# Transposing all four ds tiles of a block by DMA, and moving the plain transfers of the backward to GpSimd's queue

## The chip, the cores and the metric

The kernel runs on one core of one Trainium2 chip. The metric is the device time of one launch in microseconds (us). "Slow" here means more than 1.5% above the fastest run of the same kernel. Ratios are the mean time of one kernel's fast runs over the mean of the other's fast runs of the same rounds, so they are not quite the ratio of the medians that are quoted beside them.

## The reference

One layer with attention and a gated feed-forward part side by side, and all its gradients:

```python
xn = layernorm(x)                       # x: 1 x 2048 x 448, bf16
out = x + attention(xn, wqkv, wo)       # 16 heads of 28
        + (silu(xn @ w_gate) * (xn @ w_up)) @ w_down   # width 1792
# returned: out and the gradients of x, wqkv, wo, w_gate, w_up, w_down for a given grad_out
```

The change touches only the backward of attention. For a tile of 128 queries and 512 keys it recomputes the probabilities e, forms ds = e * (dP - delta), and needs ds in two orders: as it is for dk, and transposed for dq.

## The kernel before

The backward has 512 steps (4 groups x 2 head pairs x 4 key chunks x 16 query tiles). Four steps make a block. In each step PE makes the scores and dP, ACT makes e, DVE makes ds. Three of the four ds tiles of a block are transposed by DMA from SyncE's queue, the fourth by PE with a copy by ACT:

```python
def dst_dma(b, ds, qi):
    if qi == 0:
        dsT[b] = bk.tile([P, 4, 2, 4, P], BF16, name="dsT", bufs=3)
    SP.dma_start_transpose(out=dsT[b][:, qi]..., in_=ds[:]...)       # 128 x 1024 bf16

def ew(k):
    est[k] = kq.tile([P, 2, 512], BF16, name="e_sb", bufs=5)
    ...                                                              # ACT: exp, twice
    ds = dss[k - 1] = kq.tile([P, 2, 512], BF16, name="ds_sb", bufs=10)
    ...                                                              # DVE: multiply, twice
    if qi < 2 or qi == 2 and b < NB // 4 - 1:
        dst_dma(b, ds, qi)

def tr_unit(b):                                                      # at step 4b + 8
    for qi in (3,) if b < NB // 4 - 1 else (2, 3):
        ps = ps_b.tile([P, 8, P], BF16, name="db", bufs=3)
        for c in range(8):
            PE.transpose(ps[:, c, :], ds[...], ident_bf[:])
        ACTE.copy(out=o, in_=ps[:])                                  # DVE for qi == 2

def dq_unit(b):                                                      # at step 4b + 13
    ...                                                              # PE: 32 matmuls on dsT[b]
    if kc == 0:
        ACTE.mul(out=dq_acc[:, qsl], in_=ps[:, :256], mul=SCALE)
        return
    ...                                                              # ACT to dq_st (one buffer), GpSimd adds
```

Meanwhile the tiles for later work are loaded a little at a time, also from SyncE's queue. The filling work in PE's gaps is first the output of the layer (the "y" part, to about step 180), then the gradient of x:

```python
def drop():                       # called once a step
    ...
    while slow and credit > 0:
        _, _, o, i = slow.pop(0)
        SP.dma_start(out=o, in_=i)
        credit -= size(o)

def have(*keys):                  # what is needed now and not yet loaded
    for x in [x for x in slow if x[1] in keys]:
        slow.remove(x)
        SP.dma_start(out=x[2], in_=x[3])
```

The softmax here doesn't subtract the row's maximum and nothing guards it: scores larger than these inputs give would overflow.

Of the kernel before, what the change touches and what calls it, by code (L numbers as in the profile page):

```python
# [11 lines left out]
FP32 = mybir.dt.float32  # L12
# [26 lines left out]
def pv(hh):  # L39


    return (hh + 2) % 4
# [61 lines left out]
def kernel(  # L104
# [23 lines left out]
    PE, DVE, ACTE, POOL, SP = nc.tensor, nc.vector, nc.scalar, nc.gpsimd, nc.sync  # L128
# [419 lines left out]
    for i in range(len(chain) + LEAD):  # L548
# [4 lines left out]
        k = i - LEAD  # L553
        if k >= 0:
            b = chain[k]
# [98 lines left out]
    for t in range(4):  # L654
        run(T_unit(xnT, xn_t, t, t % 2 == 0, ps_s if t < 2 else None))
    DVE.tensor_reduce(out=r_ones[:],
                      in_=ident_f[:].rearrange("p (a b) -> p a b", b=HP)[:, :, 28:30],
# [11 lines left out]
    for c in range(3):  # L669
        k = 4 * c  # L670
# [72 lines left out]
    now = 0  # L743
# [7 lines left out]
    def size(o):  # L751
        nb = 2 if o.dtype == BF16 else 4
        for x in o.shape:
            nb *= x
        return nb

    def drop():
        nonlocal credit
        if not slow:
            credit = 0  # L760
            return
        rate, cum = RATE, 0
        for due, _, o, _ in slow:
            cum += size(o)
            rate = max(rate, (cum - credit) / max(due - now - 3, 1))
        credit += rate
        while slow and credit > 0:
            _, _, o, i = slow.pop(0)
            SP.dma_start(out=o, in_=i)
            credit -= size(o)  # L770

    def have(*keys):
        for x in [x for x in slow if x[1] in keys]:
            slow.remove(x)
            SP.dma_start(out=x[2], in_=x[3])

    def load_q(g, qc):
        t = new_q(g, qc)
# [8 lines left out]
    NB = len(steps)  # L787
    dqT, dkv, acc, dsT = {}, {}, {}, {}
    est, dss, sps, dps = {}, {}, {}, {}
# [5 lines left out]
    def store(o, i):  # L795
        held.append((now + 2, o, i))
        flush(0 if now < NB else 10 ** 9)
# [24 lines left out]
                dps[k - 1, j] = d_ps  # L822

    bk, pend = None, []

    def dst_dma(b, ds, qi):
        if qi == 0:
            dsT[b] = bk.tile([P, 4, 2, 4, P], BF16, name="dsT", bufs=3)
        SP.dma_start_transpose(out=dsT[b][:, qi].rearrange("p j kt s -> p (j kt) s"),
                               in_=ds[:].rearrange("p j k -> p (j k)"))  # L830

    def ew(k):
        if k < NB:
            est[k] = kq.tile([P, 2, 512], BF16, name="e_sb", bufs=5)
            for j in range(2):
                ACTE.activation(out=est[k][:, j], in_=sps.pop((k, j))[:], func=ACT.Exp, scale=SCALE)  # L836
        if 1 <= k <= NB:
            g, hp, kc, qc, qi = steps[k - 1]
            b = (k - 1) // 4
            ds = dss[k - 1] = kq.tile([P, 2, 512], BF16, name="ds_sb", bufs=10)  # L840
            for j in range(2):
                DVE.tensor_tensor(out=ds[:, j], in0=dps.pop((k - 1, j))[:], in1=est[k - 1][:, j], op=ALU.mult)  # L842
            if qi < 2 or qi == 2 and b < NB // 4 - 1:
                if bk is None:
                    pend.append(lambda: dst_dma(b, ds, qi))
                else:
                    dst_dma(b, ds, qi)
# [9 lines left out]
    k = n = 0  # L857
# [10 lines left out]
    bk = bwd.enter_context(tc.tile_pool(name="bk", bufs=2, reuse_waits="tile"))  # L868
# [7 lines left out]
    def late_dw(c):  # L876
# [10 lines left out]
            store(o[d0:d0 + dn, F - P:], w2[:dn, c, a])  # L887
        yield 110

    dq_acc = bk.tile([P, S // 2], FP32, name="dq_acc", bufs=1)  # L890

    def tr_unit(b):
        for qi in (3,) if b < NB // 4 - 1 else (2, 3):
            ds = dss.pop(4 * b + qi)
            ps = ps_b.tile([P, 8, P], BF16, name="db", bufs=3)
            for c in range(8):
                PE.transpose(ps[:, c, :], ds[:, c // 4, (c % 4) * P:(c % 4 + 1) * P], ident_bf[:])  # L897
            o = dsT[b][:, qi].rearrange("p j kt s -> p (j kt) s")
            if qi == 2:
                DVE.tensor_copy(out=o, in_=ps[:])  # L900
            else:
                ACTE.copy(out=o, in_=ps[:])  # L902

    def kv(k):
        g, hp, kc, qc, qi = steps[k]
        first, last = (qc == 0 and qi == 0), (qc == 3 and qi == 3)
        if first:
            acc[0] = ps_g.tile([P, 512], FP32, name="acc")
        a = acc[0]
        e = est.pop(k)  # L910
        ds = dss[k] if qi == 3 or k == NB - 2 else dss.pop(k)
        sp4 = qside[g, qc][:, 2:4, qi * P:(qi + 1) * P]
        for j in range(2):
            r = HP * pv(2 * hp + j)
            PE.matmul(a[r:r + HP, :], lhsT=sp4[:, 1, r:r + HP], rhs=e[:, j, :],  # L915
                      start=first, stop=last, tile_position=(0, r), skip_group_check=True)
        for j in range(2):
            r = HP * (2 * hp + j)
            PE.matmul(a[r:r + HP, :], lhsT=sp4[:, 0, r:r + HP], rhs=ds[:, j, :],  # L919
                      start=first, stop=last, tile_position=(0, r), skip_group_check=True)  # L920
        if last:
            if kc == 0:
                need(lambda: g == 0 or (g - 1, hp + 1, 1) in s_done)
                dkv[g, hp] = bk.tile([P, S], BF16, name=f"dkv{hp}", bufs=1)
            ACTE.activation(out=dkv[g, hp][:, kc * 512:(kc + 1) * 512], in_=a[:], func=ACT.Copy,
                            scale=(sc_a if hp == 0 else sc_b)[:, 0:1])
            if g < G - 1:
                ksl = slice(kc * 512, (kc + 1) * 512)
                store(dqkvT_d[3 * g + 1 + hp, :, ksl], dkv[g, hp][:, ksl])
            if kc == 3:  # L930
                if g < G - 1:
                    push(*[(480, lambda t8=t8: dsp_unit(g, hp + 1, t8)) for t8 in range(2)])
                elif hp == 0:
                    push(*[(480, lambda t8=t8: dsp_unit(g, hp + 1, t8)) for t8 in range(2)])

    def dq_unit(b):
        g, hp, kc, qc, _ = steps[4 * b]
        t = dsT.pop(b)
        ks = kside[g, kc][:, 2, :].rearrange("p (t r) -> p t r", r=P)
        ps = ps_g.tile([P, 512], FP32, name="genb")  # L940
        for kt in range(4):
            for par in range(2):
                for j in range(2):
                    r = HP * (2 * par + j)
                    h = HP * (2 * hp + j)
                    PE.matmul(ps[r:r + HP, :256], lhsT=ks[:, kt, h:h + HP], rhs=t[:, par::2, j, kt, :],  # L946
                              start=(kt == 0), stop=(kt == 3), tile_position=(0, r), skip_group_check=True)
        qsl = slice(qc * 256, (qc + 1) * 256)
        if kc == 0:
            ACTE.mul(out=dq_acc[:, qsl], in_=ps[:, :256], mul=SCALE)  # L950
            return
        if kc == 3 and hp == 0 and qc == 0:
            dqT[g] = bk.tile([P, 2, S // 2], BF16, name="dqT", bufs=1)
        if kc == 3 and g == G - 1:
            DVE.scalar_tensor_tensor(out=dqT[g][:, hp, qsl], in0=ps[:, :256], scalar=SCALE, in1=dq_acc[:, qsl],  # L955
                                     op0=ALU.mult, op1=ALU.add)
            return
        st = bk.tile([P, 256], FP32, name="dq_st", bufs=1)
        ACTE.mul(out=st[:], in_=ps[:, :256], mul=SCALE)  # L959
        if kc < 3:  # L960
            POOL.tensor_tensor(out=dq_acc[:, qsl], in0=dq_acc[:, qsl], in1=st[:], op=ALU.add)  # L961
            return
        POOL.tensor_tensor(out=dqT[g][:, hp, qsl], in0=dq_acc[:, qsl], in1=st[:], op=ALU.add)
        if qc == 3:
            dst = dqkvT_d[3 * g].rearrange("r (a q s) -> r a q s", q=2, s=P)
            for par in range(2):
                store(dst[64 * hp:64 * hp + 64, :, par],
                      dqT[g][64 * par:64 * par + 64, hp].rearrange("r (a s) -> r a s", s=P))
            if hp == 1:
                stream[3:3] = [(480, lambda hp=hp: dsq_unit(g, hp)) for hp in range(2)]  # L970
                at = [i for i, u in enumerate(stream) if u[1] in (dx_open, tail_open)]
                at = max(at[0] + 1, 5) if at and g != 1 else 5
                s_done.add((g, "w"))
                stream[at:at] = [(2590, lambda c=c: dwq_unit(g, c)) for c in range(4)]
# [204 lines left out]
    def push(*units):  # L1179
        stream[0:0] = units  # L1180
# [22 lines left out]
    def need(done):  # L1203
        while not done():
            for _ in stream.pop(0)[1]():
                pass
            flush(10 ** 9)
# [23 lines left out]
    for k in range(NB + 12):  # L1231
        now = k
        if k < NB:
            g, hp, kc, qc, qi = steps[k]
# [18 lines left out]
        if m == 0:  # L1253
            b = (k - 8) // 4
# [6 lines left out]
        elif m == 1:  # L1261
            b = (k - 13) // 4
# [122 lines left out]
```

## Time and profile before

| | before |
|---|---|
| median of 4 runs | 1445.2 us (1442.8 to 1448.9) |
| steps 8 to 160 of the backward | 232 us |
| steps 160 to 511 | 531 us (6.05 us a block) |
| SyncE idle in these two stretches | 0.8 and 40 us |
| transposes in these two stretches, mean time on SyncE | 113 of 1.71 us, 265 of 1.57 us |
| bytes moved by all DMA queues | 223 and 202 GB/s, at a DMA share of 1.16 and 1.08 |

A step's end is taken as the end of its second ds multiply. "SyncE idle" is the sum of the gaps of more than 0.15 us between two entries of its queue; about 0.1 us lies between most of them. The recorded texts count these gaps a little differently. SyncE does no arithmetic, so none of the engine tables shows how full its queue is. It has to be read from the timeline of SP: where each entry starts within about 0.1 us of the end of the one before, the queue has no room. The DMA share is the sum of all packets' durations over the time of 16 engines; packets of one engine can overlap, so it can pass 1.

The view of the transposes' source line in the window from 640 to 860 us (minimum/median/maximum in ns; below it, which engine waited for their data, in us and times):

```profile
L829 SPq DMA_TRANSPOSE dsT<-ds_sb x108: 1231/1420/3667, 637.2 to 858.2; - x108
...
  DVE ds_sb L842: 3.4, 4
  PE genb L946: 0.2, 1
```

Nothing waits for them to speak of. This is the baseline for what follows.

### The profile page before, as it was taken

The numbers are of one execution on the slowest core, as the hardware profiler recorded it, in microseconds if no ns is written. First come the engines' busy times: TensorE is split into PE (matmuls) and PEld (weight loads), VectorE is DVE, ScalarE is ACT, GpSimd is POOL, SyncE is SP. The second block draws the span as 40 slices with busy tenths as digits, with TensorE's granted clock in tenths as the row PEclk, the third lists the DMA queues.
The fourth block names the chain that finished last, engine by engine and source line by source line (L and its number), as shares of the span: only waits on it lengthen the run. The fifth ranks groups of instructions, "written<-read, shape, count | busy, mean of one in ns | idle before, by whom it ended". The sixth has DMA issues, their size and how long they took to land. (4 is left out here: it accounts for less than half of the span.)

```text
span 1440.1 us, 34682 instructions
## 1 busy us (share of the span) xinstructions
PE 1326.3 (92%) x12647; PEld 541.0 (38%) x12708; DVE 1151.8 (80%) x1997; ACT 1261.5 (88%) x2193; POOL 403.6 (28%) x561
## 2 busy tenths in 40 slices
PE   5889999999999999889999999999999999999996
PEld 2333333333333333333333434433443444444343
DVE  6667757666676676578998998888889999989988
ACT  5789988988889999869989989899989999989974
POOL 6464524464334454111112112201111011010006
PEclk9999999999999999989999999999999999999998
DMA  5796956796678586799999999999999999999971
GB/s 154 181 199 165 235 122 160 187 195 164 146 162 192 147 172 145 178 234 226 226 213 217 232 220 188 196 209 229 228 173 194 209 223 230 201 191 203 198 142 60
DMA packets 681179, 271.69 MB, mean 189 GB/s; under 512 B 606424, under 2 KB 655824, under 8 KB 681008
## 3 DMA queue, kind: packets, MB, share of 16 engines
q1 hardware_dynamic: 672576, 255.35, 87.1%
q0 software_dynamic: 7024, 13.82, 4.1%
q8 instruction: 100, 1.64, 0.5%
q14 instruction: 71, 0.58, 0.1%
q10 hardware_dynamic: 1408, 0.30, 0.1%
HBM read 65.09 MB, written 60.36 MB: 87 GB/s over the span
## 5 line engine op out<-in xcount | busy, mean ns | idle before, releaser
L842 DVE TENSOR_TENSOR ds_sb<-db,e_sb 128x512 bf16<-128x512 f32 x1024 | 646.8, 684 | 51.3 <-issue 21.1
L836 ACT ACTIVATE e_sb<-sb 128x512 bf16<-128x512 f32 x1024 | 554.8, 611 | 60.4 <-PE db L820 44.5
L612 ACT ACTIVATE eT<-s_w 128x1024 bf16<-128x1024 f32 x256 | 263.5, 1029 | 46.1 <-PE s_ps L609 43.1
L614 ACT ACTIVATE eT<-s_ps 128x512 bf16<-128x512 f32 x512 | 280.4, 612 | 0.0
L820 PE MATMUL db<-kd,qd 32*128 32x512 bf16 x1024 | 234.4, 384 | 8.2 <-DVE ds_sb L842 7.4
L812 PE MATMUL sb<-kd,qd 32*128 32x512 bf16 x1024 | 210.4, 387 | 5.1 <-DMA qd<-QD_d 3.3
L961 POOL TENSOR_TENSOR dq_acc<-dq_acc,dq_st 128x256 f32<-128x256 f32 x64 | 46.2, 721 | 455.4 <-ACT dq_st L959 455.4
L919 PE MATMUL acc<-ds_sb,qd 128*32 128x512 bf16 x1024 | 161.0, 391 | 0.0
L915 PE MATMUL acc<-e_sb,qd 128*32 128x512 bf16 x1024 | 158.8, 391 | 1.3 <-DVE dw_o L528 1.3
L902 ACT COPY dsT<-db 128x1024 bf16<-128x1024 bf16 x128 | 130.1, 1016 | 14.6 <-PE db L897 13.9
L380 POOL TENSOR_TENSOR nn<-nn,ag 128x512 f32<-128x512 f32 x56 | 71.2, 1271 | 252.2 <-DVE ag L378 243.7
L609 PE MATMUL s_ps<-QQ,KK 32*128 32x512 bf16 x512 | 125.4, 385 | 3.9
L1128 PE MATMUL genb<-wguT,dau_c 128*128 128x448 bf16 x448 | 117.5, 355 | 6.3 <-ACT dq_st L959 3.9
L609 PE MATMUL s_w<-QQ,KK 32*128 32x512 bf16 x512 | 100.3, 387 | 13.1 <-ACT eT L612 10.4
L812 PEld LDWEIGHTS <-qd 32*128 32x128 bf16 x1024 | 48.2, 91 | 149.4 <-issue 140.3
L421 PE MATMUL gen<-xn_t,f_sp 128*128 128x448 bf16 x416 | 91.8, 354 | 2.6 <-DVE nn L395 1.7
L421 PEld LDWEIGHTS <-f_sp 128*128 128x128 bf16 x640 | 55.7, 98 | 75.0 <-issue 31.9
L946 PE MATMUL genb<-dsT,kd 128*32 128x256 bf16 x2048 | 79.5, 275 | 1.9 <-DVE dqT L955 0.6
L897 PE MATMUL db<-ident_bf,ds_sb 128*128 128x128 bf16 x1032 | 79.4, 220 | 1.1 <-DVE ds_sb L842 1.1
L897 PEld LDWEIGHTS <-ds_sb 128*128 128x128 bf16 x1032 | 68.3, 99 | 24.1 <-issue 5.3
L451 PE MATMUL gen<-eT,VS 128*32 128x512 bf16 x1024 | 68.4, 384 | 5.5 <-DVE nn L395 3.3
L381 POOL TENSOR_TENSOR nn<-nn,tt 128x512 f32<-128x512 f32 x56 | 72.0, 1286 | 4.4
(167 smaller groups left out, 1911.0 us busy)
## 6 DMA issues: line engine op xcount, KB each, us to landing
F_d<-hda SPq DMA_DIRECT2D x56, 384.0 KB, 3.1
dau_c<-F_d SPq DMA_DIRECT2D x24, 512.0 KB, 4.4
qd<-QD_d SPq DMA_DIRECT2D x16, 512.0 KB
kd<-KD_d SPq DMA_DIRECT2D x16, 384.0 KB, 4.0
dsT<-ds_sb SPq DMA_TRANSPOSE x383, 4.3
dc<-dqkvT_d SPq DMA_DIRECT2D x12, 384.0 KB, 3.9
h_c<-F_d SPq DMA_DIRECT2D x8, 512.0 KB, 4.4
wT_d<-wT_f SPq DMA_DIRECT2D x14, 256.0 KB, 3.6
```

What stands on the lines that cost most here:

```text
L421: PE.matmul(ps[:, :D], lhsT=fsp[fc][:, t // 4, w, t % 4, :], rhs=rhs[:, t, :], start=(t == 0), stop=(t == NT - 1))
L609: PE.matmul(sp4[hh], lhsT=KK[g][r:r + HP, kt * P:(kt + 1) * P], rhs=QQ[g][r:r + HP, qsl], start=True, stop=True, tile_position=(r, 0))
L612: ACTE.activation(out=e2[0][:], in_=wide[:], func=ACT.Exp, scale=SCALE)
L614: ACTE.activation(out=e2[1][:, j], in_=sp4[2 + j], func=ACT.Exp, scale=SCALE)
L812: PE.matmul(s_ps[:], lhsT=qside[g, qc][r:r + HP, 0, qi * P:(qi + 1) * P], rhs=kside[g, kc][r:r + HP, 0, :], start=True, stop=True, tile_po ...
L820: PE.matmul(d_ps[:], lhsT=qside[g, qc][r:r + HP, 1, qi * P:(qi + 1) * P], rhs=kside[g, kc][r:r + HP, 1, :], start=True, stop=True, tile_po ...
L836: ACTE.activation(out=est[k][:, j], in_=sps.pop((k, j))[:], func=ACT.Exp, scale=SCALE)
L842: DVE.tensor_tensor(out=ds[:, j], in0=dps.pop((k - 1, j))[:], in1=est[k - 1][:, j], op=ALU.mult)
L897: PE.transpose(ps[:, c, :], ds[:, c // 4, (c % 4) * P:(c % 4 + 1) * P], ident_bf[:])
L902: ACTE.copy(out=o, in_=ps[:])
L915: PE.matmul(a[r:r + HP, :], lhsT=sp4[:, 1, r:r + HP], rhs=e[:, j, :], start=first, stop=last, tile_position=(0, r), skip_group_check=True)
L919: PE.matmul(a[r:r + HP, :], lhsT=sp4[:, 0, r:r + HP], rhs=ds[:, j, :], start=first, stop=last, tile_position=(0, r), skip_group_check=True)
```

## The change

The intent: from step 160 on (block 40, where the y part is nearly over) all four ds tiles go by DMA. This takes eight PE transposes and a copy of 1.016 us on ACT out of each block. To make room in SyncE's queue, all plain loads of the backward are issued by GpSimd from step 8. Where kc = 0, GpSimd has no addition to wait for and could run ahead with its loads, so a copy of one element ("tie") makes it wait for ACT there.

```diff
 def drop():
-            SP.dma_start(out=o, in_=i)
+            (SP if now < 8 else POOL).dma_start(out=o, in_=i)
 def have(*keys):
-            SP.dma_start(out=x[2], in_=x[3])
+            (SP if now < 8 else POOL).dma_start(out=x[2], in_=x[3])
+    PB = 40
+    def by_pe(b):
+        return (3,) if b < PB else (2, 3) if b == NB // 4 - 1 else ()
 def ew(k):
-            if qi < 2 or qi == 2 and b < NB // 4 - 1:
+            if qi not in by_pe(b):
 def tr_unit(b):
-        for qi in (3,) if b < NB // 4 - 1 else (2, 3):
+        for qi in by_pe(b):
+    tie = bk.tile([1, 1], FP32, name="tie", bufs=1)
 def dq_unit(b):
         if kc == 0:
             ACTE.mul(out=dq_acc[:, qsl], in_=ps[:, :256], mul=SCALE)
+            if now >= 8:
+                POOL.tensor_copy(out=tie[:], in_=dq_acc[0:1, qsl.start:qsl.start + 1])
```

More of the change, by code (lines that the diff above doesn't have):

```diff
@@ L910, in kv @@
         e = est.pop(k)
-        ds = dss[k] if qi == 3 or k == NB - 2 else dss.pop(k)
+        ds = dss[k] if qi in by_pe(k // 4) else dss.pop(k)
         sp4 = qside[g, qc][:, 2:4, qi * P:(qi + 1) * P]
```

## The prediction

> **What bounds the kernel now.** I read the page first, then the busy time in stretches, the groups, the timeline of SyncE's queue, and last the records of the single transposes. The page says that no engine stands out over the whole run, and where the transfers are issued:
>
> ```profile
> PE 1326.3 (92%) x12647; PEld 541.0 (38%) x12708; DVE 1151.8 (80%) x1997; ACT 1261.5 (88%) x2193; POOL 403.6 (28%) x561
> ...
> q1 hardware_dynamic: 672576, 255.35, 87.1%
> q0 software_dynamic: 7024, 13.82, 4.1%
> q8 instruction: 100, 1.64, 0.5%
> ...
> L842 DVE TENSOR_TENSOR ds_sb<-db,e_sb 128x512 bf16<-128x512 f32 x1024 | 646.8, 684 | 51.3 <-issue 21.1
> L836 ACT ACTIVATE e_sb<-sb 128x512 bf16<-128x512 f32 x1024 | 554.8, 611 | 60.4 <-PE db L820 44.5
> ...
> L902 ACT COPY dsT<-db 128x1024 bf16<-128x1024 bf16 x128 | 130.1, 1016 | 14.6 <-PE db L897 13.9
> ...
> L897 PE MATMUL db<-ident_bf,ds_sb 128*128 128x128 bf16 x1032 | 79.4, 220 | 1.1 <-DVE ds_sb L842 1.1
> ...
> dsT<-ds_sb SPq DMA_TRANSPOSE x383, 4.3
> ```
>
> L842 and L836 run twice per step of the backward, so 512 steps; the ds multiplies begin at about 618 us and end at about 1397. Counted in 20 us stretches, 302 of the 1024 multiplies have started by 840 us, so step 160 (the 320th) lies near 853 us. The changed part is therefore 352 steps, 88 blocks of four, in 544 us: **6.18 us a block**. Stretches of 100 us there:
>
> ```profile
> core 0: us, PE busy (x) PEld busy (x) DVE busy (x) ACT busy (x) POOL busy (x), PEclk, DMA share, GB/s
> ...
> 900.00:1000.00 100.00, 95.17 (x1074) 40.19 (x1066) 83.70 (x141) 92.23 (x176) 14.04 (x21) 0.98 1.15 211
> 1000.00:1100.00 100.00, 95.38 (x1094) 40.69 (x1094) 89.34 (x156) 90.41 (x170) 14.80 (x22) 0.98 1.05 198
> 1100.00:1200.00 100.00, 96.76 (x1134) 39.86 (x1126) 95.26 (x156) 94.05 (x177) 12.84 (x19) 1.00 1.12 218
> 1200.00:1300.00 100.00, 96.28 (x1116) 41.71 (x1112) 93.67 (x164) 90.42 (x168) 13.05 (x19) 1.00 1.07 202
> 1300.00:1400.00 100.00, 96.06 (x1134) 40.33 (x1130) 93.18 (x156) 89.37 (x163) 6.07 (x9) 1.00 0.99 182
> ```
>
> PE sums to 95.9% of these 500 us, DVE to 91.0%, ACT to 91.3%, and DMA packets overlap to over one engine's time each (1.08 on average). The compute engines are balanced. The busy tables leave out the queue that issues, SyncE's, and that one is nearly full too:
>
> ```profile
> 1102.54 0.57 SPq L769 DMA_DIRECT2D wguT<-wT_d  x1
> 1103.21 5.49 SPq L829 DMA_TRANSPOSE dsT<-ds_sb  x3
> 1108.75 0.57 SPq L769 DMA_DIRECT2D wguT<-wT_d  x1
> 1109.42 5.40 SPq L829 DMA_TRANSPOSE dsT<-ds_sb  x3
> 1114.87 1.01 SPq L769 DMA_DIRECT2D wguT<-wT_d  x1
> ...
> L829 SPq DMA_TRANSPOSE dsT<-ds_sb x266: 1231/1291/4112, 860.2 to 1388.2; - x133
> ```
>
> Columns of the timeline: start, length, what, count. Each entry starts within 0.1 us of the end of the one before. The last line (minimum/median/maximum in ns) shows that one transpose holds SyncE for 1.23 us at least and for up to 4.1. Its records from 855 to 1390 us: 268 transposes, mean 1.57 us; 78 plain loads, mean 0.63 us; gaps over 60 ns sum to only 37 us. **SyncE is 93% taken**, and a transpose starts a median of 1.2 us after its ds tile is ready, 5% of them 3.8 us or more. Nothing waits for it yet, because dq_unit of a block comes nine steps after the last transpose is issued. The view of SyncE's waits puts 229 us on DVE ds_sb here. I set that aside: in the records every transpose starts after its ds tile is complete.
>
> **What the Trainium skill says.** "DMA: Bandwidth & Descriptors", section "SWDGE vs HWDGE vs iDMA": a plain DMA transpose can be issued from SP or ACT only, plain copies also from GpSimd. The trace agrees: all 383 are on SPq. Same page, "Issuing engines are not separate DMA queues": transfers of all issuers share the 16 DMA engines, and spreading them saves only the issue time. Same page, "Queues, rings and completion order": an engine takes turns between rings packet by packet. The trace fits this unfavourably for the transposes: their packets have 256 B (18 ns), those of GpSimd's ring mostly 4096 B (159 ns), and while a 128 KB store of GpSimd is in flight (from 1128.9 us, say) the transpose packets fall from over 200 to under 50 in 200 ns.
>
> **The change part by part.** It *removes* 87 PE transposes of ds tiles (blocks 40 to 126): 87 x 8 transposes, 0.61 us a block in the timeline, so 53 us of PE; and 87 copies of 1.016 us, 88 us of ACT. It leaves DVE as it is. It *adds* 87 DMA transposes to SyncE. It *moves* plain loads, 78 x (0.63 + 0.05) = 53 us of SyncE after step 160 and those of steps 8 to 160 before that, to GpSimd, which is at 6 to 15% and issues one in 0.57 us (its dqkvT store). There are 32 tiny GpSimd copies more, one per dq_unit with kc = 0, which keep GpSimd from running ahead; some 10 us on an idle engine.
>
> What SyncE then needs for the 352 steps:
> - Transposes undisturbed: 1.27 us (mean of those with no plain and no instruction packet in flight) plus 0.09 us to the next: 352 x 1.36 = 479 us.
> - Instruction fetches: 16 KB packets on q8 take about 1.05 us of one DMA engine; a fit over all transposes gives 0.62 us lost for each; some 44 in this stretch: 27 us.
> - Plain bytes: about 36 MB go through in this stretch, 275 pieces of 128 KB. The same fit gives 0.25 us lost per 128 KB in SyncE's own ring and 0.42 in GpSimd's. Before, each plain load paid part of its time as issue (0.17 us per 128 KB), and 0.25 + 0.17 = 0.42: a plain byte costs the transposes the same either way. So 275 x 0.25 to 0.42 = 69 to 115 us.
>
> Sum 575 to 621 us, against 544 now: **31 to 77 us more**. As a check, the same terms for the kernel before give 268 x 1.36 + 27 + 69 + 53 = 514 us, near the 498 us that the records show (535 less 37). Per block it is 6.5 to 7.1 us for four transposes, over the 6.18 of today, and SyncE becomes the bound: transposes arrive late, dq_unit on PE waits, all behind it too. Nothing of the saving on ACT and PE reaches the end. Against this some plain bytes will pass while SyncE generates descriptors, since the bare packets of one transpose need only about 0.9 us (1136 packets a us at best, 1024 packets) of its 1.36. I take about +32 us.
>
> **The rivals.** (1) *Engine relief wins.* ACT sheds 88 us and PE 53; then DVE bounds: 91% of 544 is 495 us, which at the 96% it reaches in its best stretches is 516 us, so 28 us gained and 1418 us in all. For it: ACT and PE show hardly any gaps now, small loads (under 200 KB) in SyncE's ring delay a transpose by 0.1 us only, and the bare packets leave room. Against it: SyncE's 479 us leave only 37 us for instruction fetches and all plain traffic. (2) *A draw.* The plain loads leave SyncE and hide half in the gaps of the transposes: 479 + 27 + about 40 = 546 us, as now, 1446 us. For it: the total of DMA work is below the engines' capacity. (3) *GpSimd becomes a wait*: it issues in order, so a load that waits for its buffer holds up the dq_acc additions, and with one dq_st buffer ACT then waits. A block of slack (6 us) speaks against; it would add some 10 us.
>
> **Range and chances.** Full collision gives 1446 + 77 = 1523, the low end of the collision 1477, the draw 1446, relief 1418. I hold the collision likeliest but its size uncertain, and most of its overestimates lie toward the draw: predicted 1478, range 1432 to 1525. Slower by over 2% means above 1475: 0.52. Within 2%: 0.38. Faster by over 2%, below 1417, needs rival 1 in full: 0.10.
>
> **What would show it.** Right: 470 dsT transposes, a mean over 1.5 us each, SyncE without gaps from 860 us on; blocks of 6.5 us or more; PE at dq_unit (L946) or behind it waiting for "DMA dsT<-ds_sb", which it never did by over 0.2 us in total; ACT down by 88 us in busy time and DVE below 90% in the stretches. Wrong: transposes near 1.3 us while GpSimd's loads are in flight, blocks under 6 us, DVE at 95% or above; then the separate ring shields SyncE. Waits of ACT at dq_st for POOL would show rival 3. Steps 8 to 160 should keep their time within 3 us; if not, the moved loads alone matter.

## The result, and the profile after

The changed kernel takes **1601.6 us** (median of 4 runs, 1585.1 to 1633.4), the kernel before 1445.2. Of the four runs two are slow; the two fast ones (1585.1 and 1592.8) give a ratio of **1.099** (1.093 to 1.105). The direction was as predicted, the size far outside the range. The profile fell into a slow run (span 1608.7 us, some 1.4% above the fast ones). What follows is read from it where the fast runs of the experiments show the same; the profile's sizes hold for a slow run.

From the page of the kernel after:

```profile
PE 1369.7 (85%) x12012; PEld 512.6 (32%) x12012; DVE 1151.4 (72%) x1997; ACT 1197.3 (74%) x2106; POOL 487.4 (30%) x710
...
q1 hardware_dynamic: 730064, 228.47, 77.9%
q0 software_dynamic: 20560, 63.52, 17.0%
...
L846 DVE TENSOR_TENSOR ds_sb<-db,e_sb 128x512 bf16<-128x512 f32 x1024 | 647.7, 685 | 215.6 <-DMA dsT<-ds_sb 70.3
...
L951 PE MATMUL genb<-dsT,kd 128*32 128x256 bf16 x2048 | 101.1, 296 | 98.8 <-DMA dsT<-ds_sb 90.7
...
dsT<-ds_sb SPq DMA_TRANSPOSE x470, 4.5
```

The work is what was intended: 470 transposes, 50 MB moved from queue q1 to q0. But two groups now stand idle in front of the transposed tiles. DVE loses 70 us because the ten ds buffers don't come free until their transposes have read them; PE loses 91 us at dq because the transposes have not landed. These two lines are the reversal of the two lines shown for the kernel before.

Two stretches of 100 us of the kernel after (columns as in the prediction's table):

```profile
1000.00:1100.00 100.00, 79.32 (x756) 26.64 (x753) 66.06 (x105) 65.64 (x131) 19.61 (x32) 0.90 1.14 212
1200.00:1300.00 100.00, 83.38 (x796) 27.21 (x789) 76.46 (x126) 66.14 (x129) 18.87 (x32) 0.89 1.13 201
```

DVE and ACT fell from about 90 to between 66 and 76; the DMA share is 1.13 to 1.14 with no more bytes per second than before. And a line of SyncE's timeline of this kernel:

```profile
1148.80 51.62 SPq L833 DMA_TRANSPOSE dsT<-ds_sb  x27
```

The view of the transposes' source line, from 900 us on (minimum/median/maximum in ns):

```profile
L833 SPq DMA_TRANSPOSE dsT<-ds_sb x350: 1232/1298/8651, 899.6 to 1554.8; - x175
```

27 transposes, nothing else, in 51.6 us: 1.91 us each, though the plain loads are gone from this queue. The median is 1.30 us, so it is the tail that costs; one transpose held SyncE for 8.7 us.

By steps the time went here (profiled spans, 168.6 us more in all; the two fast runs are 144 us slower than the kernel before, so some 25 us of this table belong to the slow run):

| | before | after | difference |
|---|---|---|---|
| to step 8 | 632.0 | 636.0 | 4 |
| steps 8 to 160 | 231.8 | 269.2 | 37 |
| steps 160 to 511 | 531.0 | 648.0 | 117 |
| rest | 45.2 | 55.5 | 10 |

In steps 160 to 511 SyncE is idle for 3.4 us in all; 345 transposes of 1.775 us and 0.09 us between them fill the 648 us. In steps 8 to 160, where the number of transposes has not changed, their mean rose from 1.71 to 2.13 us.

### The profile page after: what moved, and what is told of

Its sections match the earlier page's. It is cut to its first block, busy times and chain, and to the rows that moved or that the text cites. A ratio compares the mean times of both kernels' runs of the same rounds, so it can differ in the third digit from the quotient of the medians.

```text
span 1608.7 us, 33351 instructions
## 1 busy us (share of the span) xinstructions
PE 1369.7 (85%) x12012; PEld 512.6 (32%) x12012; DVE 1151.4 (72%) x1997; ACT 1197.3 (74%) x2106; POOL 487.4 (30%) x710
## 5 line engine op out<-in xcount | busy, mean ns | idle before, releaser
L820 PE MATMUL db<-kd,qd 32*128 32x512 bf16 x1024 | 249.1, 408 | 42.3 <-DVE ds_sb L846 41.9
L812 PE MATMUL sb<-kd,qd 32*128 32x512 bf16 x1024 | 220.8, 411 | 5.0 <-DMA qd<-QD_d 3.3
L951 PE MATMUL genb<-dsT,kd 128*32 128x256 bf16 x2048 | 101.1, 296 | 98.8 <-DMA dsT<-ds_sb 90.7
L924 PE MATMUL acc<-ds_sb,qd 128*32 128x512 bf16 x1024 | 170.8, 411 | 0.3 <-DVE ds_sb L846 0.2
L920 PE MATMUL acc<-e_sb,qd 128*32 128x512 bf16 x1024 | 168.1, 411 | 1.3 <-DVE dw_o L528 1.3
L1135 PE MATMUL genb<-wguT,dau_c 128*128 128x448 bf16 x448 | 121.2, 385 | 3.1 <-ACT dq_st L966 2.0
L951 PEld LDWEIGHTS <-kd 128*32 128x32 bf16 x2048 | 61.0, 101 | 154.0 <-issue 66.1
L966 ACT ACTIVATE dq_st<-genb 128x256 f32<-128x256 f32 x88 | 34.1, 388 | 96.0 <-PE genb L951 95.7
L957 POOL COPY tie<-dq_acc 1x1 f32<-1x1 f32 x32 | 5.6, 173 | 221.8 <-ACT dq_acc L955 221.8
```

The lines of the kernel that those rows point to most:

```text
L812: PE.matmul(s_ps[:], lhsT=qside[g, qc][r:r + HP, 0, qi * P:(qi + 1) * P], rhs=kside[g, kc][r:r + HP, 0, :], start=True, stop=True, tile_po ...
L820: PE.matmul(d_ps[:], lhsT=qside[g, qc][r:r + HP, 1, qi * P:(qi + 1) * P], rhs=kside[g, kc][r:r + HP, 1, :], start=True, stop=True, tile_po ...
L920: PE.matmul(a[r:r + HP, :], lhsT=sp4[:, 1, r:r + HP], rhs=e[:, j, :], start=first, stop=last, tile_position=(0, r), skip_group_check=True)
L924: PE.matmul(a[r:r + HP, :], lhsT=sp4[:, 0, r:r + HP], rhs=ds[:, j, :], start=first, stop=last, tile_position=(0, r), skip_group_check=True)
L951: PE.matmul(ps[r:r + HP, :256], lhsT=ks[:, kt, h:h + HP], rhs=t[:, par::2, j, kt, :], start=(kt == 0), stop=(kt == 3), tile_position=(0, r ...
L1135: PE.matmul(ps[:, :D], lhsT=d[:, i // 2, i % 2, tsl], rhs=dxs["w", fq][:, i // 2, i % 2, :], start=(i == 0), stop=(i == n - 1))
```

## The experiments

A ring is here the queue in which the transfers of one issuer wait for the DMA engines. The page lists GpSimd's as q0 software_dynamic, SyncE's as q1 and ScalarE's as q10, both hardware_dynamic; hence the software ring and the hardware rings below. Three theories were to be told apart. **A**, the prediction's: SyncE's time to issue transposes is the bound, and plain bytes delay them whichever ring carries them. **B**: the software ring of GpSimd is the culprit, the fourth transpose alone is nearly free. **D**: the DMA engines cannot carry more of this mix; SyncE is only held by a full ring, and its fullness is a mirror of theirs. All runs gave right results except the one marked.

### The two halves of the change, each alone

Run e1 keeps the plain loads on SyncE:

```diff
-            (SP if now < 8 else POOL).dma_start(out=o, in_=i)      # both places
+            SP.dma_start(out=o, in_=i)
-            if now >= 8:
-                POOL.tensor_copy(out=tie[:], ...)
```

> Only the ds half of the change: four ds tiles by DMA from step 160, plain loads stay on SyncE, no tie copy. Theory A (SyncE's transposes are the bound and plain bytes delay them whichever ring carries them): steps 160 to 511 need 345 x 1.36 = 469 us of bare transposes, 27 us for instruction fetches, 70 us for plain bytes and 53 us of plain issue, about 620 us against 531 before, so about 1535 us in all; steps 8 to 160 stay at 232 us. Theory B (the software ring of GpSimd is the culprit, the fourth transpose is nearly free): within 20 us of the kernel before, 1445 to 1465 us.

Measured: **1534.6 us** (1533.5 to 1537.2; before 1441.5), ratio 1.065 (1.063 to 1.066). Steps 8 to 160 took 229.6 us, steps 160 to 511 took 617 us with SyncE idle for 3.2 us. Theory B in its pure form falls: the fourth tile by DMA costs 93 us with no plain transfer on GpSimd's ring but its usual stores. Two 150 us stretches of this run:

```profile
950.00:1100.00 150.00, 123.92 (x1235) 43.91 (x1227) 110.03 (x185) 103.18 (x205) 16.89 (x25) 0.92 1.13 218
1100.00:1250.00 150.00, 125.67 (x1251) 42.24 (x1247) 119.59 (x200) 101.65 (x200) 16.83 (x25) 0.94 1.13 207
```

The DMA columns read 1.13 and 207 to 218 GB/s, as in the kernel after, while every compute engine has room. The transposes of this run from 900 us on, to be held against the pairs of e5 below:

```profile
L833 SPq DMA_TRANSPOSE dsT<-ds_sb x321: 1237/1294/3687, 898.6 to 1469.3; - x161
...
  PE genb L950: 43.3, 32
  DVE ds_sb L846: 9.7, 14
```

The loads, which stand in the same queue, came late here too: after step 160 PE waited some 29 us for them.

Run e2 keeps three tiles by DMA and moves the loads:

```diff
-        return (3,) if b < PB else (2, 3) if b == NB // 4 - 1 else ()
+        return (2, 3) if b == NB // 4 - 1 else (3,)
```

> Only the moved loads: plain transfers on GpSimd from step 8 with the tie copy, three ds tiles by DMA throughout as before. Theory A: steps 8 to 160 take about 269 us as in the changed kernel (232 before); from step 160 SyncE needs 265 x 1.39 + 30 + 268 x 0.51 = 535 us, the same as the 531 of before; in all 1480 to 1490 us. Theory B (the software ring is the whole loss): most of the loss is here, 1550 us or more. If the moved loads cost nothing by themselves: 1445 us.

Measured: **1503.6 us** (1498.8 to 1510.2), ratio 1.043 (1.040 to 1.047). Steps 8 to 160 took 260 us (232 before), steps 160 to 511 took 557 us (531). So the moved loads cost some 62 us by themselves. The two halves, 93 + 62 = 155 us, account for the whole loss (the fast runs of the changed kernel lie 144 us above the kernel before), with some 11 us in both. The source line of e2 from 640 to 860 us, to be held against that of the kernel before:

```profile
L833 SPq DMA_TRANSPOSE dsT<-ds_sb x100: 1231/1756/6781, 639.0 to 858.1; - x100
...
  DVE ds_sb L846: 17.7, 9
```

With the same number of transposes to do, the median rose from 1.42 to 1.76 us and the longest from 3.7 to 6.8 us. DVE began to wait for its buffers. After step 160 SyncE was idle for 46 us in e2, no less than in the kernel before, and the steps still took 26 us more; a full queue alone doesn't explain that part.

### A second hardware ring instead of GpSimd's

Run e3 is e2 with the loads on ScalarE (and no tie); run e6 is the whole change with the loads on ScalarE:

```diff
-            (SP if now < 8 else POOL).dma_start(out=o, in_=i)
+            (SP if now < 8 else ACTE).dma_start(out=o, in_=i)
```

> Plain transfers from step 8 issued from ScalarE (a hardware ring of its own with packets of 1 to 4 KB instead of GpSimd's software ring), three ds tiles by DMA throughout, no tie copy. If it is the software ring's 4 KB packets that starve the 256 B transpose packets, transposes stay near 1.5 us here and SyncE gains idle time; ScalarE pays some 110 issues of 0.6 us in its queue: 1440 to 1480 us. If any second ring starves them alike, transposes average over 1.8 us in steps 8 to 160 and the time is at or above that of the moved loads alone.

> The changed kernel with its plain transfers issued from ScalarE instead of GpSimd, no tie copy. It completes the table of (three or four tiles) x (plain on SyncE, GpSimd, ScalarE). Transposes bound either way; without plain issues on SyncE (53 us) and without the software ring: steps 160 to 511 need 345 x (1.29 + 0.09) + 30 + about 90 = 595 us against 617 with the plain on SyncE and 648 on GpSimd, so about 1505 to 1525 us. If the ring matters only together with three tiles: 1590 us as the changed kernel.

Measured: e3 **1451.3 us** (1447.5 to 1458.6), ratio 1.007 (1.003 to 1.011); e6 **1541.4 us** (1530.5 to 1542.9), ratio 1.069 (1.065 to 1.073). The table is now complete (ratios to the kernel before):

| plain loads issued by | three tiles by DMA | four from step 160 |
|---|---|---|
| SyncE | 1 | 1.065 |
| ScalarE | 1.007 | 1.069 |
| GpSimd | 1.043 | 1.099 |

The fourth tile costs 6 to 7% in the first two rows and 5% in the third. Taking the loads off SyncE's queue gains nothing in any column, even on a second hardware ring. In e6 SyncE was idle for 12 us of steps 160 to 511, which took 617.5 us, the same as in e1 with 47 us less of plain issue on SyncE. That already speaks against the issue time as the bound: what SyncE no longer spent on issuing loads, the transposes took longer (1.66 us on average, 1.52 in e1). It is not a clean test by itself: after step 160 ScalarE stood idle for 88 us in front of its loads there, for 9 us in e3. e6 was expected faster than e1 and is not; theory A mis-sized it.

### Two tiles to one transpose

A transpose of 2048 columns takes less issue time than two of 1024. e4 does it in the kernel before (first two tiles of a block), e5 with all four tiles by DMA from step 160; loads stay on SyncE.

```diff
-            ds = dss[k - 1] = kq.tile([P, 2, 512], BF16, name="ds_sb", bufs=10)
+            if qi % 2 == 0:
+                dpair[0] = kq.tile([P, 2, 2, 512], BF16, name="ds_sb", bufs=5)
+            ds = dss[k - 1] = dpair[0][:, qi % 2]
+            SP.dma_start_transpose(out=dsT[b][:, qi - 1:qi + 1]..., in_=pair[:]...)   # at qi == 1; in e5 from step 160 also at qi == 3
```

> The kernel before with the first two ds tiles of a block transposed by one instruction of 2048 columns (a forward transpose of that size took 1.6 to 1.9 us, two of 1024 take 2.7 with the gap), the third alone, the fourth on PE. Theory A with the issue time of a transpose as the bound: SyncE needs 1.0 us a block less, it has idle time in steps 8 to 160 (2.8 us before), and those steps get a little faster: 1430 to 1445 us. Rival D (the DMA engines themselves, not SyncE's issue, are full): the pair holds SyncE as long as two singles, nothing changes, 1445 us, or it gets worse by the later start of the first tile.

> All four ds tiles by DMA from step 160, but two tiles to one transpose instruction (2048 columns), plain loads on SyncE. A pair took 1.9 us where nothing else was in flight, against 2.6 for two singles. If the time that SyncE needs to issue a transpose is the bound (theory A as predicted): 176 pairs x 2.0 = 350 us, some 95 us of delays and 53 us of plain issue, about 500 us, less than the 531 us of before, so the relief of ACT and PE shows: 1415 to 1450 us. If the flow of the packets through the shared DMA engines is the bound and SyncE is only held by a full ring (theory D): pairs of over 3 us, steps 160 to 511 near the 617 us of the singles, about 1520 to 1535 us.

Measured: e4 1445.1 us, ratio 1.001 (0.998 to 1.004). e5 **1518.7 us** (1516.1 to 1522.9), ratio 1.055 (1.053 to 1.057). The pairs of e5 from 900 us on:

```profile
L840 SPq DMA_TRANSPOSE dsT<-ds_sb x163: 1316/3112/5114, 900.2 to 1459.9; - x163
...
  DVE ds_sb L856: 59.6, 38
  PE genb L961: 34.0, 24
```

After step 160 a transpose of e5, nearly all of them pairs, held SyncE for 2.99 us on average, as long as two singles of e1 (2 x 1.52), although the few pairs of e4 with no other packet beside them took 1.7 to 2.1 us. Steps 160 to 511 took 599 us against 617 for the singles of e1; if issue had been the bound it would have been about 500. In e4, too, SyncE's idle time did not grow (0.4 and 41 us; 0.8 and 40 before). **Theory D holds in the main**: SyncE is held until its ring takes more, and the ring is not emptied faster. The ring itself is not in the records; that it is full is read from these times. Joining the issues saved those 18 us and no more.

The records also show where D is too simple. In e1 147 of the 348 transposes after step 160 had no plain and no instruction packet beside them and took 1.29 us on average, the undisturbed time: for these SyncE's own pace counted. In e5 61 of the 174 pairs ran so, in 2.20 us instead of the 2.67 of two such singles and a gap; with two or more 128 KB pieces beside it a pair took 3.4 us. And whether the engines themselves are the limit, or something behind them on the packets' way, no run here tells. That few of them had nothing to do fits: in e1's steps 160 to 511 fewer than eight packets were in flight for 2% of the time.

### What the relief of ACT and PE is worth

e7 (the gradient of wqkv is off): from step 160 the fourth tile is not transposed at all and dq reads the other three. Its output is wrong, which doesn't matter for the time.

```diff
-            if qi not in by_pe(b):
+            if qi not in by_pe(b) and not (qi == 3 and b >= PB):
-    rhs=t[:, par::2, j, kt, :]
+    rhs=t[:, par:par + 2, j, kt, :] if PB <= b < NB // 4 - 1 else t[:, par::2, j, kt, :]
```

> Wrong result on purpose: from step 160 the fourth ds tile is neither transposed on PE nor by DMA, and dq reads the other three instead (same matmuls). Plain loads on SyncE. This is the relief alone: ACT and PE lose the transposes, DMA keeps what it had. If ACT and PE were at their bound and DVE is next (rival 1): 28 us less, 1410 to 1420 us. If the DMA flow already limits at three tiles, or DVE does: 1430 to 1441 us; then there was little to win even with a free transpose. The output dq part is wrong.

Measured: **1417.7 us** (1415.9 to 1423.0), ratio 0.985 (0.982 to 0.988). So the hope behind the change was sound: without that work the kernel is 22 us faster.

```profile
1100.00:1250.00 150.00, 142.29 (x1535) 51.09 (x1533) 146.52 (x242) 124.50 (x245) 19.04 (x28) 0.99 1.17 216
```

DVE is busy for 146.5 of 150 us there: the next bound, as rival 1 said (from 950 to 1100 us it is 132.7, so not everywhere). But the DMA columns read 1.17 and 216 GB/s, and SyncE's idle time after step 160 fell from 40 to 10 us. Even with three tiles little room is left once the compute engines go faster.

### A small dose

e11 uses only the slack that SyncE had: in the kernel before, the fourth tile goes by DMA in every fourth block from block 47 (20 blocks).

```diff
-        return (3,) if b < PB else (2, 3) if b == NB // 4 - 1 else ()
+        return (2, 3) if b == NB // 4 - 1 else () if b >= PB and b % 4 == 3 else (3,)   # PB = 44, loads on SP
```

> The kernel before with the fourth ds tile by DMA in every fourth block from block 47 (20 blocks), plain loads on SyncE. SyncE had 40 us without work after step 160, the run without the fourth transpose gained 22 us for 87 tiles. If the DMA flow is the bound only once that slack is used up: 20 tiles x 0.25 us = 5 us less, 1435 to 1438 us against 1440. If every transpose added is paid for at once: 20 x 1 us more, 1455 to 1465 us.

Measured with five rounds: 1443.8 us (1437.4 to 1447.2), before 1441.8, ratio 1.003 (0.999 to 1.006). SyncE's idle time after step 160 fell to 6.5 us and the step time stayed (532 us). The slack was used up, and neither the gain of 5 us, which lies outside the interval, nor a loss shows. No version here beats the kernel before.

### The tie copy

e8 is the changed kernel without the tie.

```diff
-            if now >= 8:
-                POOL.tensor_copy(out=tie[:], in_=dq_acc[0:1, qsl.start:qsl.start + 1])
```

> The changed kernel without the 32 tie copies. If they only keep GpSimd from running ahead: loads bunch up in the stretches with kc = 0, transposes stall longer, 1590 to 1640 us, that is equal to or above the changed kernel's 1590. If the tie itself holds GpSimd and so the loads (rival 3): well below, under 1570 us.

Measured: 1590.0 us (1576.6 to 1617.8, one of four slow), ratio 1.101 (1.096 to 1.106), the same as with the tie. The tie neither helps nor hurts. GpSimd's order is not the cause either: from 630 us on PE, DVE and ACT of the kernel after wait for GpSimd for 1.4 us in all, and for one of its loads once, for 5.1 us.

### Why GpSimd's ring carries less

The records give the bytes moved by all queues in the same steps:

| run | steps 8 to 160: GB/s (share) | steps 160 to 510 |
|---|---|---|
| before | 223 (1.16) | 202 (1.08) |
| e1, four tiles, loads on SyncE | 226 (1.14) | 208 (1.13) |
| e5, four tiles in pairs, loads on SyncE | 227 (1.15) | 215 (1.12) |
| e6, four tiles, loads on ScalarE | 218 (1.19) | 209 (1.16) |
| e7, no fourth tile, loads on SyncE | 224 (1.16) | 210 (1.14) |
| e3, three tiles, loads on ScalarE | 226 (1.17) | 197 (1.09) |
| e2, three tiles, loads on GpSimd | 202 (1.16) | 191 (1.10) |
| e12, as e2, pieces of 128 KB | 217 (1.18) | 188 (1.11) |
| e13, as e2, pieces of 64 KB | 205 (1.20) | 194 (1.13) |
| after, four tiles, loads on GpSimd | 197 (1.14) | 197 (1.13) |

Where SyncE had hardly a gap, 208 to 227 GB/s were carried with the loads on a hardware ring, and about 197 to 202 with whole loads on GpSimd's; cut into pieces of 128 KB (e12, explained below) they reached 217 in steps 8 to 160. The share alone does not tell the mix: at the moments of e1 after step 160 with no plain and no instruction packet within 0.3 us (48% of that time), the transposes by themselves moved 212 GB/s at a share of 1.18. The data packets of GpSimd's ring have 4150 B on average (1540 B on the others' rings), those of the transposes 256 B. Four runs looked at whether packet size or bursts of whole loads explain the difference. e9 is e3 and e10 the kernel before with the spilled activations laid out so that their loads read rows of 4096 B; e12 and e13 are e2 with every load cut into pieces of at most 128 or 64 KB.

```diff
-    F_d = dram.tile([4, P, NFC, 3, 512], BF16)                       # e9, e10
+    H_d = dram.tile([4, P, NFC, 512], BF16)
+    A_d = dram.tile([4, P, NFC, 2, 512], BF16)

-            (SP if now < 8 else POOL).dma_start(out=o, in_=i)        # e12, e13
+            emit(o, i)             # halves o and i until a piece has at most 128 (64) KB, then POOL
```

> As the run with plain transfers on ScalarE and three tiles by DMA, but the spilled activations are stored so that the loads of the backward read contiguous rows of 4096 B; this ring's packets then have mostly 4096 B as those of GpSimd's ring do, instead of 1528 B on average. (The forward has 56 small stores more, which may cost a few us before step 0; the steps are compared.) If large packets, taken in turn with the 256 B packets of the transposes, are what makes GpSimd's ring worse: steps 8 to 160 go from 232 us to 255 us or more, and the flow falls from 226 to about 200 GB/s. If it is something else in the software ring: steps 8 to 160 stay within 5 us of 232.

> The kernel before with the same contiguous 4096 B rows, plain loads on SyncE in the transposes' own ring. Fewer, larger packets take no less engine time in the records (four of 1024 B 236 ns, one of 4096 B 204 to 227), so no gain is expected in the steps: 1440 to 1450 us.

> The moved loads alone (three tiles by DMA, plain on GpSimd with the tie copy), each load cut into pieces of at most 128 KB. Packets stay at 4096 B; GpSimd needs 0.56 us a piece, so a load enters the engines at 234 GB/s at most instead of all at once. If bursts of whole loads are what stalls the transposes on GpSimd's ring: steps 8 to 160 fall from 260 us towards 240 and the time towards 1465 us. If bursts don't matter: 260 us and 1500 us as with whole loads.

> The same with pieces of at most 64 KB: packets of 2048 B (as in GpSimd's 64 KB stores) and at most 117 GB/s. If the packet size of GpSimd's ring against the 256 B packets of the transposes is the cause: steps 8 to 160 near 235 us, whole time near 1450 us, and clearly better than with 128 KB pieces. If neither packet size nor bursts are: 260 us or more, 1500 us or more, since the number of issues grows eightfold.

| run | median us | ratio | steps 8 to 160 | steps 160 to 511 |
|---|---|---|---|---|
| e3, ScalarE | 1451.3 | 1.007 | 232 | 539 |
| e9, ScalarE, 4096 B rows (one of four slow) | 1457.8 | 1.011 (1.006 to 1.016) | 244 | 535 |
| e10, SyncE, 4096 B rows | 1439.0 | 1.001 (0.997 to 1.004) | 230 | 529 |
| e2, GpSimd | 1503.6 | 1.043 | 260 | 557 |
| e12, GpSimd, 128 KB pieces | 1485.7 | 1.028 (1.022 to 1.034) | 242 | 568 |
| e13, GpSimd, 64 KB pieces | 1490.9 | 1.035 (1.032 to 1.038) | 254 | 554 |

e9 raised the mean packet in steps 8 to 160 from 1376 to 2279 B and these steps became 12 us longer, but e6, whose steps 8 to 160 are those of e3 up to the last, had 238 us there; so 6 to 12 us, from one profile each. After step 160, where many 2048 B packets became 4096 B ones as well, nothing got slower. On SyncE's own ring large packets are harmless (e10). Pieces of 128 KB gain 18 us of e2's 62 in whole time; in the profile the gain lies in steps 8 to 160 alone. In e13 the packets did not shrink as intended (3899 B on average: a 64 KB load is sent in 16 packets of 4096 B), so it says nothing on packet size. **What stays open** is therefore why GpSimd's ring disturbs the transposes more than ScalarE's: bursts have a part in it, large packets alone do not explain it.

## Why the prediction was right or wrong

**SyncE's queue is full and the transposes come late: right in what is seen, for the most part wrong in the cause.** The wait of PE at dq for the transposed tiles, the 470 transposes, the mean over 1.5 us (1.775), SyncE without gaps, DVE below 90%: all came as listed. But the step "352 x 1.36 = 479 us" took the issue time as the scarce thing. The pairs show that halving the issues leaves SyncE as busy as before (523 us of transposes after step 160, 529 in e1). The scarce thing, for the most part, is what is carried of 256 B transpose packets beside plain ones, 208 to 227 GB/s. The profile before had it in sight: in steps 8 to 160 SyncE had no gap at 223 GB/s. The prediction noted the share of 1.08 and passed over it, since the bare packets of a transpose need only 0.9 us of its 1.36. Beside plain packets that room was not to be had.

**Three readings of the profile before: wrong.** The 302 multiplies that the prediction took to have started by 840 us were added up from 20 us windows, and a multiply counts in each window that it touches; 291 had started. So the steps after 160 took 531 us and not 544, and the same sum, 575 to 621 us, stands 44 to 90 us above today and not 31 to 77. The "gaps over 60 ns" of SyncE sum to 60 us; 37 are left when the usual 0.09 us at each entry are taken off, so 93% counts these as taken. And at 1128.9 us no transpose packet was in flight, behind a plain load of SyncE's own ring; the fall that is described comes at the next store of GpSimd, at 1130.4 us.

**Undisturbed transposes and instruction fetches: right.** A fit over the transposes of the kernel after gives 1.29 us (1.27 predicted, both with some 0.09 between) and 0.62 us for each of some 50 times that an instruction packet ran beside a transpose (0.62, 44).

**The plain bytes: the mis-sized term, and the first step that failed the number.** Predicted were 275 x 0.25 to 0.42 = 69 to 115 us; the same fit to the kernel after gives 268 pieces of 128 KB at 0.51 us, 137 us. "A plain byte costs the transposes the same either way" held for a second hardware ring (e3, e6) and failed for GpSimd's. With this term the sum gives what was measured after step 160: 345 x 1.38 + 30 + 137 = 643 us, against 648.

**Steps 8 to 160 "should keep their time within 3 us": wrong, 37 us in the slow profile; the second step that failed the number.** The sum of SyncE's needs was made only for the steps after 160. The same records show that SyncE was idle for only 0.8 us of steps 8 to 160 in the kernel before. Moving the loads to a ring that carries less had to be paid there at once; e2 pays 28 us there.

**"Against this some plain bytes will pass while SyncE generates descriptors": a discount that did not come.** The working gave 31 to 77 us and the estimate was drawn to the low end, toward the draw. The fourth tile alone, without any moved load, cost 93 us; the expectation of e1 without that discount and from 531 us was 1535 us, and 1534.6 were measured. That this sum of issue times came out right is partly luck, since the pairs refute it as the cause. But even the undiscounted 1446 + 77 = 1523 us lies 79 us below the result. Most of that is in the two steps above, 137 instead of 115 us and 37 instead of none; 14 us more came before step 8 and after step 511.

**The rivals.** Relief was worth 22 us where 28 were estimated, and DVE was the next bound, as said; it could not be had with the transpose still to be done: without it SyncE's queue had 10 us left (e7). The draw is what the small dose shows (e11). GpSimd as a wait was not seen. A fourth one was not named: TensorE's granted clock (as a share of full speed) fell from 0.985 to 0.93 to 0.94. It falls in every run in which PE waits much (0.957 in e1, 0.963 in e2), while SyncE has hardly a gap in the stretches with four tiles, so I take it for a consequence; no run shows that by itself.

## What to carry to other kernels

A queue that issues DMA can be full because its issues take long or because the engines behind it are full. Joining two issues into one helps to tell these apart: if the joined one holds the queue as long as the two, although it is shorter when nothing else runs, the issues are not what is scarce. Before moving work from a compute engine to DMA, find a stretch with the DMA engines saturated, read the GB/s of that mix there, and compare it with what the change will ask for: here the 107 MB that steps 160 to 511 moved before and 80 more transposes of 0.26 MB, in the 509 us of the run without a fourth tile, ask for 252 GB/s (an estimate from e7 and the transposes counted) where 208 to 215 were to be had in that stretch (e1, e5, e6). And don't expect a transfer to cost the same on GpSimd's ring as on a hardware ring where many transposes are in flight.

## What the Trainium skill lacked or had wrong

- "DMA: Bandwidth & Descriptors", section "Issuing engines are not separate DMA queues", says that transfers of all issuers run on the same engines and that issuing from several saves only issue time. It does not say that the choice can cost: with transposes in flight the kernel took 4.3% longer with the same loads on GpSimd (e2), and 0.7% with ScalarE (e3, which also has 43 us of issue time on ScalarE).
- The same page, section "Latency and other measured facts", gives transposes 261 GB/s in one kernel. It has no figure for transposes beside plain transfers: here 208 to 227 GB/s in all with hardware rings, 197 to 202 with whole loads on GpSimd, each at a DMA share of 1.1 to 1.2.
- No page gives the time that a transpose from SBUF to SBUF holds its issuing queue on trn2 in us ("VectorE: DVE Perf Modes" has a time for one tile of 128 x 128 by DMA, "DMA: Bandwidth & Descriptors" has cycles for "previous generations"): here 1.23 us at least for 128 x 1024 bf16, 1.32 at least for 128 x 2048, and a median of 3.1 us for the latter in e5.
- "DMA: Bandwidth & Descriptors", section "Queues, rings and completion order", names row 14 for the runtime's refills. In this trace instruction packets stand on q8 as well, of 16 KB and about 1.05 us each. No page says what they cost other transfers: by the fit some 0.6 us for a transpose beside one.
